# Pooled keys of a fused attention and ResMLP kernel: TensorE products replaced by transposing transfers and VectorE column sums from the third batch on

## The chip, the cores and the metric

The kernel runs on one core of one Trainium2 chip. A core has five engines, each with its own instruction queue: TensorE (PE; its weight loads, PEld, overlap its products), VectorE (DVE), ScalarE (ACT), GpSimd (POOL) and SyncE (SP), which here only issues transfers. Each queue is worked off in its order, and an instruction whose inputs are not there holds up what is queued behind it. Transfers are moved by 16 DMA engines. Those that SP (and at a few places ACT) issues stand in the profile under queue q1, those that POOL issues under q0. The metric is device time in microseconds (us), lower is better.

## The reference

Attention over pooled keys and values, and behind it a ResMLP block on the same tokens. There are 8 batches, 8 heads, 576 tokens and head size 64, in float32; eight neighbouring tokens of k and v are averaged, which leaves 72 groups.

```python
# attention: q, k, v are (8, 8, 576, 64)
k_p = k.reshape(B, H, 72, 8, D).mean(axis=3)
v_p = v.reshape(B, H, 72, 8, D).mean(axis=3)
scores = scale * np.matmul(q, k_p.transpose(0, 1, 3, 2))
attn = softmax(scores)                       # written out: max, exp, sum
x = np.matmul(attn, v_p)                     # then (B, S, H * D)
# ResMLP: d_model 512, hidden 2048
a1 = alpha1 * x + beta1
tok = np.einsum('ts,bsd->btd', w_tok, a1)
u = x + lam * tok
a2 = alpha2 * u + beta2
out = u + lam * (np.maximum(a2 @ w_ch1, 0.0) @ w_ch2)
```

## The kernel before

**Blocks.** All tokens of all batches are cut into 36 chunks of 128 tokens, and four chunks make a block, so there are nine blocks n = 0 to 8 (the loop at line 1127). Block n does the two large products of the MLP on its 512 tokens: `mlp_A` (line 838: 16 pieces, each four products of 128x512, then ReLU on ACT) and, from block 2 on, `product` (line 945, with half-width columns and sums of hidden parts, `hidden_sum` on DVE) and `gather` (line 976, DVE). Between these pieces the attention and the token mixing of batch b = n + 1 are spread out (`attention(b)`, line 1076).

**Order.** Nothing schedules this at run time. Each step of a block is put in a list with a number, the list is sorted by it (line 1205), and the steps are written to the engines' queues in that order. One unit is about one piece of `mlp_A` on TensorE; a block has some 30 units. So a step with 28.5 stands near the end of its block, one with 0.2 at the start of it.

**Keys of a batch, from batch 1 on.** `load_k` (line 275) loads four heads at a time: 512 tokens a head, four neighbouring tokens in one partition. `sum_k` (line 368) adds the four on POOL with two instructions, `k_raw` (line 372) and `k_bf` (line 374), and writes the sum twice side by side, so that two copies of a head fill 128 columns. `att_K` (line 624) then pools pairs of partitions and transposes at once by products with a constant matrix: for each half of the heads (u = 0, 1) four products of line 632 and, for the last 64 tokens, two of line 638, into a PSUM bank of the ring `gp` (six banks, used in turn for nearly everything). DVE copies the bank to SBUF as `kp` (line 644). In the list, `sum_k` stands at -0.9 and 0.3 and `att_K` at 4.1 and 6.1.

**The last 64 tokens** of q and k come with `load_rem` (line 328). `cast_rem` (line 351, on POOL, at 23.1 of the block before) makes bfloat16 copies `rem_q` and `rem_k`; where batches are loaded into reused memory a one-column DVE memset (line 355) stands ahead of them. `att_Frem` (line 603, at 26.72) transposes `rem_q` by a transfer into one of two buffers `rem_qT`.

**Scores.** `att_S4` (line 689) stands at 6.3 for u = 0 and at 13.6 for u = 1. Its products (lines 700 and 707) need `kp`, the transposed queries `qT` (a transfer, line 584) and `rem_qT`. ACT takes the exponentials (line 729, scale 0.125), `att_AV` (line 733) multiplies with the pooled v, and DVE divides (lines 749 and 751), which frees the bank.

**Other users of the SP queue.** `mix_uT` (line 813) transposes each finished chunk `u_bf` to `u_fm` by a transfer (line 820). A block with an odd batch has a fifth such chunk, near unit 27.4; it belongs to the block after the next. `store` (line 880) writes four chunks of the output, at 27.2 (two) and 29.2 (two). `load_v` (line 340, at 3.5 and 7.5), `load_rem` and `load_k` (near 21) fetch the next batch. POOL issues the loads of `q_bf` (line 266) at 0.4 and 0.5 for batches 4 to 7, so just behind `sum_k`.

**Memory reused.** `wt_bf` (the token weights as loaded) is dead once its transposes are made; `scale_w2` (line 898) takes its place for the first of four parts of the scaled second MLP weight. `kpT_pool` is used by batch 0 alone.

Of the kernel before, what the change touches and what calls it, by code (L numbers as in the profile page):

```python
# [7 lines left out]
FP = mybir.dt.float32  # L8
F16 = mybir.dt.float16
BF = mybir.dt.bfloat16  # L10
AF = mybir.ActivationFunctionType
ALU = mybir.AluOpType
AX = mybir.AxisListType

P = 128
SPG = 72
DM = 512
# [171 lines left out]
def direct(  # L189
# [19 lines left out]
    nc = tc.nc  # L209
    ctx.enter_context(tc.manual_schedule())  # L210
    B, H, S, D = q.shape

    const = ctx.enter_context(tc.tile_pool(name="const", bufs=1))
    work = ctx.enter_context(tc.tile_pool(name="work", bufs=1))
# [3 lines left out]
    def gp(name):  # L218
        return psA.tile([P, 512], FP, tag="gp", name=name)
# [29 lines left out]

        nc.vector.tensor_reduce(out=fine, in_=every, op=ALU.min, axis=AX.X)  # L250

    st1 = {}

    def new_batch(b):
        st1[b] = {"qT": [None] * 2, "ET": [None] * H, "raw": [None] * 2, "q": [None] * 2,
# [94 lines left out]

    def cast_rem(b, eng, copy=None, behind=None):
        raw = st1[b]["rem_raw"]
        rq = work.tile([P, 2, 2, D], BF, tag="rem_q", bufs=2, name="rem_q")
        if behind is not None:
            behind.memset(rq[:, 0, 0, 0:1], 0.0)
        rk = work.tile([P, 2, 2 if b else 3, D], BF, tag="rem_k", bufs=2, name="rem_k")
        (copy or eng.tensor_copy)(out=rq.rearrange("p c h d -> p h c d"), in_=raw[:, 0])
        twice = [raw[:, 1, :, c].unsqueeze(2).to_broadcast((P, 2, 2, D)) for c in range(2)]
        if b:
            eng.tensor_tensor(out=rk, in0=twice[0], in1=twice[1], op=ALU.add)  # L360
        st1[b]["rem"] = rq, rk

    def cast_rem_k(eng):
        raw, rk = st1[0]["rem_raw"], st1[0]["rem"][1]
# [3 lines left out]
    def sum_k(b, u, eng):  # L368

        raw = st1[b]["raw"][u]  # L370
        bf = work.tile([P, 4, 2, D], BF, tag="k_bf", bufs=2, name="k_bf")
        eng.tensor_tensor(out=raw[:, :, 0:2], in0=raw[:, :, 0:2], in1=raw[:, :, 2:4], op=ALU.add)  # L372
        twice = [raw[:, :, c].unsqueeze(2).to_broadcast((P, 4, 2, D)) for c in range(2)]
        eng.tensor_tensor(out=bf, in0=twice[0], in1=twice[1], op=ALU.add)  # L374
        st1[b]["k"][u] = bf


    wt_bf = const.tile([P, 5 * S + 64], BF, tag="wt_bf", name="wt_bf")
# [63 lines left out]
    load_wtok()  # L442

    vp1_pool, kpT_pool, kp_pool, ET_pool = [], [], [], []
    for i in range(4):
        if i < 2:
            t = const.tile([SPG, 4, 66], F16, tag=f"vp1_{i}", name=f"vp1_{i}")
            nc.vector.memset(t, 8.0)
            vp1_pool.append(t)
            t = const.tile([P, 2, 4, SPG], BF, tag=f"kpT_{i}", name=f"kpT_{i}")  # L450
            nc.vector.memset(t, 0.0)
            kpT_pool.append(t)
            kp_pool.append(const.tile([P, 4, SPG], BF, tag=f"kp_{i}", name=f"kp_{i}"))
    for i in range(2):
        t = const.tile([SPG, 4, S + 64], F16, tag=f"ET_{i}", name=f"ET_{i}")
        nc.vector.memset(t[:, :, S:], 1.0)
# [9 lines left out]
                            in1=pool_v[0:32, 1:16:2], op=ALU.add)  # L466
# [136 lines left out]
    def att_Frem(b, copy=None):  # L603

        st = st1[b]
        st["rem_qT"] = work.tile([P, 2, P], BF, tag="rem_qT", bufs=2, name="rem_qT")
        if copy is None:
            nc.sync.dma_start_transpose(out=st["rem_qT"],
                                        in_=st["rem"][0].rearrange("p c h d -> p (c h d)"))
            return  # L610
        ps_q = gp("ps_qr").bitcast(BF)
        for c in range(2):
            nc.tensor.transpose(out=ps_q[:, 128 * c:128 * c + 128],
                                in_=st["rem"][0][:, c].rearrange("p h d -> p (h d)"),
                                identity=identity_bf)
        copy(out=st["rem_qT"], in_=ps_q[:, 0:256].rearrange("p (c t) -> p c t", c=2))
# [7 lines left out]
    def att_K(b, u, copy):  # L624

        st = st1[b]
        ps_kp = gp("ps_kp")
        kp = ps_kp[:, 0:4 * SPG].rearrange("p (h g) -> p h g", g=SPG)
        n, nr = (1, 1) if b else (4, 2)
        for h in range(4):  # L630
            for c in range(n):
                nc.tensor.matmul(  # L632
                    out=kp[:, h, 0:64],
                    lhsT=st["k"][u][:, h, c:c + 2].rearrange("p a d -> p (a d)"),
                    rhs=pool_main, start=(c == 0), stop=(c == n - 1))
        for hh in range(2):
            for c in range(nr):
                nc.tensor.matmul(
                    out=kp[:, hh:4:2, 64:72],
                    lhsT=st["rem"][1][:, hh, c:c + 2].rearrange("p a d -> p (a d)"),  # L640
                    rhs=pool_rem.rearrange("p (g u r) -> p u r g", r=2, u=2)[:, u],
                    start=(c == 0), stop=(c == nr - 1))
        if b:
            copy(out=kp_pool[u], in_=kp)
            return
        for a in range(2):
            rows = slice(64 * a, 64 * a + 64)
            (copy or (nc.scalar.copy, nc.vector.tensor_copy)[a])(
                out=kpT_pool[u][rows, a], in_=kp[rows])

    def first_V(b, u, copy=nc.vector.tensor_copy):

# [36 lines left out]
    def att_S4(b, u):  # L689

        st = st1[b]
        qT, kp, rest = st["qT"][u], kp_pool[u], st["rem_qT"]
        lo = [psB.tile([P, DM], FP, tag="ch", bufs=2, name="ps_s") for _ in range(2)]
        hi = [gp("ps_s") for _ in range(2)]
        r = [gp("ps_r")[0:SPG, 0:128].rearrange("p (h i) -> p h i", i=64) for _ in range(2)]

        def main(i):
            for a in range(2):
                rows = slice(64 * a, 64 * a + 64)
                nc.tensor.matmul(  # L700
                    out=(hi if i > 1 else lo)[a][0:SPG, 256 * (i % 2):256 * (i % 2) + 256],
                    lhsT=kp[rows, i, :], rhs=qT[rows, 2 * i:2 * i + 2, :])

        def rests(i):
            for a in range(2):
                rows = slice(64 * a, 64 * a + 64)
                nc.tensor.matmul(  # L707
                    out=r[a][:, i // 2], lhsT=kp[rows, i + a, :],
                    rhs=rest[rows, :, 2 * u + i // 2::4].rearrange("p c i -> p i c"))

        pairs = ((lo, 0), (hi, 2)) if u else ((hi, 2), (lo, 0))
        main(pairs[0][1])
        rests(pairs[0][1])
        main(pairs[0][1] + 1)
        main(pairs[1][1])
        rests(pairs[1][1])
        main(pairs[1][1] + 1)
        ET = ET_pool[u]
        for i in range(4):
            st["ET"][4 * u + i] = ET[:, i]  # L720

        def exp(k):
            if k < 2:
                o, i = ET[:, k::2, 512:S], r[k]
            else:
                a, (pair, h) = k % 2, pairs[k // 2 - 1]
                o = ET[:, h:h + 2, 256 * a:256 * a + 256]
                i = pair[a][0:SPG, :].rearrange("p (h i) -> p h i", i=256)
            nc.scalar.activation(out=o, in_=i, func=AF.Exp, bias=0.0, scale=0.125)  # L729

        st["exp", u] = exp

# [158 lines left out]

    FIRST = 2
    HALF = DM // 2
    wino = {}

    w2l = {}

    def scale_w2(g, i):

        if g not in w2l:  # L900
            if g == 1:
                both = const.tile([P, 6 * DM], BF, tag="vecs", name="w2_l")
                w2l[1] = both[:, 0:4 * DM].rearrange("p (i d) -> p i d", d=DM)
                wino["spare"] = both[:, 4 * DM:].rearrange("p (j t) -> p j t", t=HALF)
            else:
                w2l[g] = const.tile([P, 4, DM], BF, tag=("wt_bf", None, "w2_0", "w2_1")[g],
                                    name="w2_l")
        nc.vector.tensor_tensor(out=w2l[g][:, i], in0=w2[g][:, i], in1=lam_bc, op=ALU.mult)

    def weight_sum(i, g):  # L910
# [92 lines left out]
    more_constants()  # L1003
    keep_warm(1)
    att_Frem(0, nc.scalar.copy)
    keep_warm(1)
    spread_lam()
    double_k(0)
    att_K(0, 0, None)
    spread_al1(0)  # L1010
    bias_row(0)
# [64 lines left out]
    def attention(b):  # L1076


        first = b == 1
        todo = []  # L1080
# [11 lines left out]
            todo.append((25.6 if first else 23.1, lambda: cast_rem(b + 1, nc.gpsimd, behind=None if first else nc.vector)))  # L1092
            todo.append((26.72 if b > 1 else 26.22, lambda: att_Frem(b + 1)))
        for u in range(2):
            todo.append((3.6 + 0.1 * u if first else -0.9 + 1.2 * u,
                         lambda u=u: sum_k(b, u, nc.gpsimd)))
            todo.append((7.0 + 2.3 * u if first else 4.1 + 2.0 * u,
                         lambda u=u: att_K(b, u, nc.vector.tensor_copy)))
        for u in range(2):
            at = (9.0 if first else 6.3, 13.6)[u]  # L1100
            todo.append((at, lambda u=u: att_S4(b, u)))
# [3 lines left out]
            for i, dt in enumerate((2.9, 3.4, 4.6, 5.1) if u else early):  # L1105
                h = 4 * u + i
                todo.append((at + dt, lambda h=h: att_AV(b, h)))
                if i % 2:
                    eng = nc.gpsimd if h == 5 or first and h < 5 else nc.vector
# [17 lines left out]
    for n in range(NBLK):  # L1127
        todo = []
# [60 lines left out]
        b = n + 1  # L1189
# [61 lines left out]
```

## Time and profile before

The median of three runs is 333.19 us (333.13 to 333.4). The profiled execution took 332.3 us; the span from its first to its last instruction is 330.6 us, and times in the views count from the span's start. The granted TensorE clock reads 1.00 in it.

| what | instructions | one, ns | busy, us |
|---|---|---|---|
| DVE, all | 490 | | 235.5 (71% of the span) |
| ACT, all | 322 | | 175.5 (53%) |
| POOL, all | 110 | | 95.6 (29%) |
| L632 products `ps_kp` of `k_bf` | 56 | 193 | 3.9 |
| L638 products `ps_kp` of `rem_k` | 36 | 178 | 3.4 |
| L644 DVE `kp` <- `ps_kp`, 128x288 | 14 | 451 | 6.3 |
| L372 POOL `k_raw`, 128x512 | 14 | 1338 | 18.7 |
| L374 POOL `k_bf`, 128x512 | 14 | 1318 | 18.5 |
| L820 SP transposing issue `u_fm` | 32 | 1212 (median) | |
| L584 SP transposing issue `qT` | 12 | 1284 (median) | |
| L608 SP transposing issue `rem_qT` | 6 | 1196 (median) | |

Products are pipelined, so the mean duration of one is not what it takes of TensorE's time; that is read from the distance between starts. The duration of an SP issue is the time that the SP queue is held, not the time until the data has landed. q1 moved 32.67 MB in 52,236 packets, q0 12.40 MB in 13,824.

In the profiled execution the blocks n = 1 to 7 begin on TensorE at 67.7, 102.9, 137.8, 171.5, 206.4, 240.0 and 274.9 us; the block that begins at 137.8 us carries the attention of batch 4.

### The profile page before, as it was taken

How to read it: one execution, taken by the hardware profiler on the slowest of the kernel's cores; microseconds unless marked ns; L12 is line 12 of the kernel's file. 1: busy time of each engine (PE TensorE's matmuls, PEld its weight loads, DVE VectorE, ACT ScalarE, POOL GpSimd, SP SyncE). 2: the span in 40 equal slices, each digit the busy share in tenths (PEclk: the TensorE clock that was granted, in tenths of full speed). 3: DMA queues.
4: the chain of work that ended last, by engine and by line, in shares of the span. 5: the costliest groups of instructions: out<-in, count | busy, mean ns of one | idle time of the engine just before them, and what ended most of it. 6: DMA issues, size and time to landing. Idle time of an engine off the chain costs nothing.

```text
span 330.6 us, 6522 instructions
## 1 busy us (share of the span) xinstructions
PE 324.9 (98%) x2528; PEld 208.9 (63%) x2528; DVE 235.5 (71%) x490; ACT 175.5 (53%) x322; POOL 95.6 (29%) x110
## 2 busy tenths in 40 slices
PE   8999999999999999999999999999999999999995
PEld 3667764455545576656775677557755866586584
DVE  6674389999589969776967796878688783265263
ACT  2775989458323852387128812782268225803710
POOL 8769738301256011700290028102610200000000
PEclk9999999999999999999999999999999999999999
DMA  8999999959894982499549934995340044003003
GB/s 119 193 219 270 268 210 249 207 145 124 165 255 68 221 203 59 76 227 165 164 119 201 171 125 89 207 195 157 65 136 2 0 65 143 2 0 129 2 32 97
DMA packets 66618, 45.83 MB, mean 139 GB/s; under 512 B 34541, under 2 KB 57205, under 8 KB 66586
## 3 DMA queue, kind: packets, MB, share of 16 engines
q1 hardware_dynamic: 52236, 32.67, 42.6%
q0 software_dynamic: 13824, 12.40, 22.9%
q8 instruction: 20, 0.33, 0.4%
q10 hardware_dynamic: 526, 0.34, 0.3%
q14 instruction: 12, 0.10, 0.1%
HBM read 38.30 MB, written 9.44 MB: 144 GB/s over the span
## 4 chain that ended last, share of the span: by engine, by line
PE 98%; DVE 1%; issue 0%; ACT 0%
PE ps_h L849 38%; PE ps_w L972 26%; PE ps_tok L801 12%; PE ps_ch L869 8%; PE ps_av L743 3%; PE ps_s L700 2%; PE ps_warm L792 2%; PE ps_kp L632 1%; PE ps_r L707 1%; PE ps_av L747 1%; PE ps_q L589 1%; PE ps_sc L680 0%; PE ps_rs L528 0%; PE ps_w L516 0%; PE ps_uT L825 0%; PE ps_v L659 0%
## 5 line engine op out<-in xcount | busy, mean ns | idle before, releaser
L849 PE MATMUL ps_h<-u_fm,w 128*128 128x512 bf16 (+2 forms) x608 | 133.7, 369 | 0.2 <-DVE bias_cols L852 0.2
L856 ACT ACTIVATE H<-ps_h,bias_cols 128x512 bf16<-128x512 f32 x144 | 98.1, 688 | 56.5 <-PE ps_h L849 55.5
L849 PEld LDWEIGHTS <-w 128*128 128x128 bf16 x608 | 65.8, 114 | 49.7 <-issue 2.2
L972 PEld LDWEIGHTS <-H 128*128 128x128 bf16 x560 | 53.4, 98 | 10.9 <-DVE u_sb L990 1.2
L809 ACT CAST u_bf<-u_sb 128x512 bf16<-128x512 f32 x32 | 19.8, 618 | 70.0 <-issue 39.9
L972 PE MATMUL ps_w<-w_l,H 128*128 128x256 bf16 x448 | 53.6, 273 | 0.0
L990 DVE TENSOR_TENSOR u_sb<-u_sb,ps_w 128x512 f32<-128x512 f32 x54 | 36.3, 682 | 17.0 <-PE ps_w L972 17.0
L765 POOL TENSOR_TENSOR xs<-x_tm,lamal_bc 128x512 bf16<-128x512 f32 x12 | 15.9, 1330 | 108.8 <-DVE x_tm L751 108.6
L801 PE MATMUL ps_tok<-xs,wtT 128*128 128x512 bf16 (+3 forms) x200 | 44.9, 381 | 0.1
L805 DVE TENSOR_TENSOR u_sb<-x_tm,ps_tok 128x512 f32<-128x512 f32 (+1 forms) x40 | 27.3, 683 | 9.9 <-PE ps_tok L801 9.9
L751 DVE TENSOR_TENSOR x_tm<-ps_av,recs 128x320 f32<-128x320 f32 x64 | 31.5, 492 | 2.6
L729 ACT ACTIVATE ET<-ps_s 72x512 f16<-72x512 f32 x56 | 32.3, 591 | 0.0
L801 PEld LDWEIGHTS <-wtT 128*128 128x128 bf16 (+3 forms) x200 | 17.4, 100 | 16.2 <-issue 1.1
L749 DVE RECIPROCAL recs<-ps_av 128x5 f32<-128x5 f32 x64 | 12.1, 188 | 16.7 <-PE ps_av L747 16.6
L670 DVE TENSOR_TENSOR v_u<-v_u 72x1024 f32<-72x1024 f32 (+1 forms) x24 | 22.7, 948 | 0.2
L972 PE MATMUL ps_w<-w_t,h_s 128*128 128x256 bf16 x168 | 22.6, 273 | 0.0
L869 PEld LDWEIGHTS <-H 128*128 128x128 bf16 x128 | 11.9, 98 | 13.7 <-issue 0.4
L372 POOL TENSOR_TENSOR k_raw<-k_raw 128x512 f32<-128x512 f32 x14 | 18.7, 1338 | 1.2 <-PE ps_ch L869 0.7
L972 PEld LDWEIGHTS <-h_s 128*128 128x128 bf16 x168 | 16.4, 98 | 4.1
L941 DVE TENSOR_TENSOR H<-H,H 128x1024 bf16<-128x1024 bf16 x14 | 9.7, 690 | 12.8 <-ACT H L856 12.7
L374 POOL TENSOR_TENSOR k_bf<-k_raw 128x512 bf16<-128x512 f32 x14 | 18.5, 1318 | 1.1
L743 PEld LDWEIGHTS <-ET 72*128 72x128 f16 x256 | 14.0, 97 | 6.0 <-DVE vp L664 0.3
(153 smaller groups left out, 369.3 us busy)
## 6 DMA issues: line engine op xcount, KB each, us to landing
out_dram<-u_sb SPq DMA_DIRECT2D x29, 256.0 KB
k_raw<-in_k_dram SPq DMA_DIRECT2D x12, 512.0 KB
v_u<-in_v_dram SPq DMA_DIRECT2D x12, 512.0 KB
q_bf<-in_q_dram POOLq DMA_DIRECT2D x16, 256.0 KB, 7.4
w<-in_moe_w_ch_dram POOLq DMA_DIRECT2D x6, 512.0 KB, 12.9
out_dram<-u_sb SPq DMA_DIRECT2D x11, 128.0 KB
w<-in_moe_w_ch_dram POOLq DMA_DIRECT2D x1, 1024.0 KB, 14.3
k_raw<-in_k_dram POOLq DMA_DIRECT2D x2, 512.0 KB, 16.7
```

Of the source, the lines that this page charges most:

```text
L670: nc.vector.tensor_tensor(out=out, in0=t[:, :, 0:width], in1=t[:, :, width:2 * width], op=ALU.add)
L729: nc.scalar.activation(out=o, in_=i, func=AF.Exp, bias=0.0, scale=0.125)
L743: nc.tensor.matmul(out=av[:, odd + c, :], lhsT=ET[:, m0:m0 + 128], rhs=vp1[:, h % 4, :])
L751: nc.vector.tensor_tensor(out=x[:, 1 - odd:6 - odd, dd:dd + D], in0=av[:, :, 0:64], in1=rec.unsqueeze(2).to_broadcast((P, 5, D)), op=ALU.mult)
L801: nc.tensor.matmul(out=ps_tok[p0:p1], lhsT=wtT[0:kk, at, P * c:P * c + p1 - p0], rhs=xs_pool[i][0:kk, sc, :], start=(sc == 0), stop=(sc == 4))
L805: nc.vector.tensor_tensor(out=s["u"][p0:p1, :], in0=x[p0:p1, 1 + c if c < 4 else 5 - 5 * i, :], in1=ps_tok[p0:p1, 0:DM], op=ALU.add)
L809: nc.scalar.copy(out=s["u_bf"], in_=s["u"])
L849: nc.tensor.matmul(out=ps_h[:, t0:t1 + one], lhsT=w1_of(cc, j), rhs=rhs, start=(cc == 0), stop=(cc == 3))
L856: nc.scalar.activation(out=H4[n, j // 4][:, j % 4, :], in_=ps_h, func=AF.Relu, bias=bias_cols[:, j:j + 1], scale=1.0)
L869: nc.tensor.matmul(out=ps, lhsT=H_of(n, j)[:, 128 * m:128 * m + 128], rhs=(w2l if n else w2)[j // 4][:, j % 4, :], start=(j == 0), stop=(j ...
L972: nc.tensor.matmul(out=ps, lhsT=stat(j), rhs=moving(j), stop=(j == 7), start=(first and (pp == 0 or alone) and j == 0), skip_group_check=True)
L990: nc.vector.tensor_tensor(out=o, in0=o, in1=banks[key, "both"], op=ALU.add)
```

## The change

From batch 2 on, `att_K` is no longer called. In its place:

- `att_KT` transposes the four-token sums `k_bf` of half the heads (128x512) by a transfer on SP, into the old `kpT_pool` memory. u = 0 stands at 28.5 of the block before, u = 1 at 0.2 of the batch's own block.
- `att_Ksum` (DVE, at 4.3 and 6.3) adds neighbouring columns of it and writes `kp`.
- `cast_rem` writes the last tokens of q and k side by side, and one transfer in `att_Frem` transposes both (512 columns, where it was 256) into a single buffer beside the scaled weight in the old `wt_bf` memory.
- `att_Krest` (POOL, two instructions at 0.25) adds the eight last-token groups into `kp` for all heads.
- `sum_k` of batch b + 1 now stands at 28.1 and 28.2 of the block before. On POOL's queue it keeps its place behind `cast_rem`; `att_Krest` comes between it and the issue of the `q_bf` loads.
- The pooled keys are sums and not means, and the factor 1/8 goes into the scale of the exponentials.

In the queue of SP the transposes of `att_KT` stand so: at the change to batches 4 and 6 behind three stores (two of them of half a chunk) and the fifth `u_fm`, then two stores, then u = 1; at the change to batches 5 and 7 behind two stores, then two stores, then u = 1; at the change to batch 3 right behind `att_Frem`, then two stores, then u = 1; at the change to batch 2 between the two transposes of `qT`, and u = 1 behind two stores. In all of these the loads of v follow.

```diff
     def cast_rem(b, eng, copy=None, behind=None):
-        rq = work.tile([P, 2, 2, D], BF, tag="rem_q", bufs=2, name="rem_q")
+        both = work.tile([P, 5, 2 * D], BF, tag="rem_qk", bufs=2, name="rem_qk")
...
     def att_Frem(b, copy=None):
+        if copy is None:
+            both = wino["rem_T"].rearrange("p (x t) -> p x t", t=P)
+            nc.sync.dma_start_transpose(out=both, in_=st["rem"][2])
+            st["rem_qT"], st["rem_kT"] = both[:, 0:2], both[:, 2:4]
+            return
...
+    def att_KT(b, u):
+        nc.sync.dma_start_transpose(out=quads_of(u),
+                                    in_=st1[b]["k"][u].rearrange("p h a d -> p (h a d)"))
+
+    def att_Krest(b, eng):
+        pairs = st1[b]["rem_kT"].rearrange("p e (r i a) -> p (e r) i a", i=2, a=8)
+        half = wino["half"].bitcast(FP).rearrange("p (e a) -> p e a", a=8)
+        eng.tensor_tensor(out=half, in0=pairs[:, :, 0], in1=pairs[:, :, 1], op=ALU.add)
+        eng.tensor_tensor(
+            out=kp_both[:, :, 64:72].rearrange("p (a e) r -> p e r a", e=2),
+            in0=half[:, :, 0:4].rearrange("p (e r) a -> p e r a", e=2),
+            in1=half[:, :, 4:8].rearrange("p (e r) a -> p e r a", e=2), op=ALU.add)
+
+    def att_Ksum(b, u):
+        quads = quads_of(u).rearrange("p h (g i) -> p h g i", i=2)
+        nc.vector.tensor_tensor(out=kp_pool[u][:, :, 0:64], in0=quads[:, :, :, 0],
+                                in1=quads[:, :, :, 1], op=ALU.add)
...
-            nc.scalar.activation(out=o, in_=i, func=AF.Exp, bias=0.0, scale=0.125)
+            nc.scalar.activation(out=o, in_=i, func=AF.Exp, bias=0.0,
+                                 scale=0.125 if b == 1 else 0.125 / 8)
...
         for u in range(2):
-            todo.append((3.6 + 0.1 * u if first else -0.9 + 1.2 * u,
-                         lambda u=u: sum_k(b, u, nc.gpsimd)))
-            todo.append((7.0 + 2.3 * u if first else 4.1 + 2.0 * u,
-                         lambda u=u: att_K(b, u, nc.vector.tensor_copy)))
+            if first:
+                todo.append((3.6 + 0.1 * u, lambda u=u: sum_k(b, u, nc.gpsimd)))
+                todo.append((7.0 + 2.3 * u, lambda u=u: att_K(b, u, nc.vector.tensor_copy)))
+            else:
+                todo.append((4.3 + 2.0 * u, lambda u=u: att_Ksum(b, u)))
+            if b < B - 1:
+                todo.append((28.1 + 0.1 * u, lambda u=u: sum_k(b + 1, u, nc.gpsimd)))
+        if b < B - 1:
+            todo.append((28.5, lambda: att_KT(b + 1, 0)))
+        if not first:
+            todo.append((0.2, lambda: att_KT(b, 1)))
+            todo.append((0.25, lambda: att_Krest(b, nc.gpsimd)))
```

More of the change, by code (lines that the diff above doesn't have):

```diff
@@ L250, in count_in_range @@
         nc.vector.tensor_reduce(out=fine, in_=every, op=ALU.min, axis=AX.X)
-    st1 = {}
+    st1, wino = {}, {}
     def new_batch(b):
@@ L352, in cast_rem @@
         raw = st1[b]["rem_raw"]
-        rq = work.tile([P, 2, 2, D], BF, tag="rem_q", bufs=2, name="rem_q")
+        both = work.tile([P, 5, 2 * D], BF, tag="rem_qk", bufs=2, name="rem_qk")
         if behind is not None:
-            behind.memset(rq[:, 0, 0, 0:1], 0.0)
-        rk = work.tile([P, 2, 2 if b else 3, D], BF, tag="rem_k", bufs=2, name="rem_k")
+            behind.memset(both[:, 0, 0:1], 0.0)
+        rq = both[:, 0:2].rearrange("p c (h d) -> p c h d", h=2)
+        flat = both.rearrange("p x d -> p (x d)")
+        n = 4 if b else 6
+        rk = flat[:, 4 * D:(4 + n) * D].rearrange("p (h a d) -> p h a d", h=2, a=n // 2)
         (copy or eng.tensor_copy)(out=rq.rearrange("p c h d -> p h c d"), in_=raw[:, 0])
@@ L360, in cast_rem @@
             eng.tensor_tensor(out=rk, in0=twice[0], in1=twice[1], op=ALU.add)
-        st1[b]["rem"] = rq, rk
+        st1[b]["rem"] = rq, rk, flat[:, 0:8 * D]
     def cast_rem_k(eng):
@@ L444, in direct @@
     vp1_pool, kpT_pool, kp_pool, ET_pool = [], [], [], []
+    kp_both = const.tile([P, 8, SPG], BF, tag="kp", name="kp")
     for i in range(4):
@@ L452, in direct @@
             kpT_pool.append(t)
-            kp_pool.append(const.tile([P, 4, SPG], BF, tag=f"kp_{i}", name=f"kp_{i}"))
+            kp_pool.append(kp_both[:, 4 * i:4 * i + 4])
     for i in range(2):
@@ L605, in att_Frem @@
         st = st1[b]
+        if copy is None:
[3 more added lines that the diff above has]
+            return
         st["rem_qT"] = work.tile([P, 2, P], BF, tag="rem_qT", bufs=2, name="rem_qT")
[L607 to L610, printed above, removed]
         ps_q = gp("ps_qr").bitcast(BF)
@@ L649, in att_K, with quads_of @@
                 out=kpT_pool[u][rows, a], in_=kp[rows])
+    def quads_of(u):
+        return kpT_pool[u].rearrange("p a h g -> p (a h g)")[:, 0:512].rearrange(
+            "p (h t) -> p h t", t=P)
+    def att_KT(b, u):
[13 more added lines that the diff above has]
+                                in1=quads[:, :, :, 1], op=ALU.add)
     def first_V(b, u, copy=nc.vector.tensor_copy):
@@ L893, in direct @@
     HALF = DM // 2
-    wino = {}
     w2l = {}
@@ L904, in scale_w2 @@
                 wino["spare"] = both[:, 4 * DM:].rearrange("p (j t) -> p j t", t=HALF)
-            else:
-                w2l[g] = const.tile([P, 4, DM], BF, tag=("wt_bf", None, "w2_0", "w2_1")[g],
-                                    name="w2_l")
+            elif g == 0:
+                both = const.tile([P, 4 * DM + 6 * P], BF, tag="wt_bf", name="w2_l")
+                w2l[0] = both[:, 0:4 * DM].rearrange("p (i d) -> p i d", d=DM)
+                wino["rem_T"] = both[:, 4 * DM:4 * DM + 4 * P]
+                wino["half"] = both[:, 4 * DM + 4 * P:]
+            else:
+                w2l[g] = const.tile([P, 4, DM], BF, tag="w2_%d" % (g - 2), name="w2_l")
         nc.vector.tensor_tensor(out=w2l[g][:, i], in0=w2[g][:, i], in1=lam_bc, op=ALU.mult)
```

## The prediction

> **What bounds the kernel now.** I read the page's shares first, then the chain of work that ended last around one change of batch, then the queues of SP and DVE there, and last what the DMA engines moved in the same microseconds. Part 1 and part 4 of the page:
>
> ```profile
> PE 324.9 (98%) x2528; PEld 208.9 (63%) x2528; DVE 235.5 (71%) x490; ACT 175.5 (53%) x322; POOL 95.6 (29%) x110
> PE 98%; DVE 1%; issue 0%; ACT 0%
> ```
>
> TensorE is busy for 98% of the span and is 98% of the chain. What is taken from its queue shortens the run, and a wait put into it lengthens the run, one for one, unless something covers it. The chain from 137 to 148 us (start, length, what), where batch 4's attention begins:
>
> ```profile
> 137.84 4.32 PE ps_h L849 x20
> 142.16 0.12 PE ps_kp L632 x4
> 142.27 0.05 PE ps_kp L638 x2
> 142.32 1.74 PE ps_h L849 x8
> 144.06 0.12 PE ps_kp L632 x4
> 144.18 0.04 PE ps_kp L638 x2
> 144.22 0.23 PE ps_s L700 x2
> ```
>
> The pooling products hold TensorE for 0.16 us twice per batch, and the first score product follows at 144.22 us. There are no gaps, so nothing waits for keys now: `k_bf` was done on POOL by 137.4 us. The SP timeline there (start, time that the queue is held), and POOL's issue of the q loads:
>
> ```profile
> 136.85 1.21 SPq L889 DMA_DIRECT2D out_dram<-u_sb  x2
> 138.10 0.58 SPq L885 DMA_DIRECT2D out_dram<-u_sb  x1
> 138.78 1.61 SPq L820 DMA_TRANSPOSE u_fm<-u_bf  x1
> 140.49 1.02 SPq L885 DMA_DIRECT2D out_dram<-u_sb  x2
> ```
> ```profile
> 137.38 1.57 POOL L266 DMA_DIRECT2D q_bf<-in_q_dram  x2
> ```
>
> The transpose of `u_bf` issued at 138.78 us is of the size of a k transpose, 128x512. When does its data move? The DMA view of 139 to 143 us, then of 143 to 146 us (packets, MB, share of 16 engines):
>
> ```profile
> DMA packets 829, 0.69 MB, mean 174 GB/s; under 512 B 48, under 2 KB 637, under 8 KB 829
> q0 software_dynamic: 605, 0.30, 67.8%
> q1 hardware_dynamic: 224, 0.39, 36.3%
> ```
> ```profile
> DMA packets 1091, 0.55 MB, mean 184 GB/s; under 512 B 560, under 2 KB 995, under 8 KB 1091
> q1 hardware_dynamic: 640, 0.33, 65.3%
> q0 software_dynamic: 451, 0.22, 58.6%
> ```
>
> A 128x512 transpose is 128 KB, and the small packets come in lots that fit 512 packets of 256 B for each. Up to 143 us only 48 small ones passed; the 560 came from 143 to 146 us. So this transpose needed about 7 us from issue to the end of its data, behind the stores ahead of it in q1 and beside the q loads of q0. Without such traffic (133.6 to 136.2 us) 1083 small packets passed in 2.6 us at 50.1% of the engines: 0.6 to 0.7 us of pure transfer for 512. At the change to batch 6 it is the same: from 207.3 to 211.8 us q0 moved 1020 packets and q1 99, 40 of them small; the `u_fm` issued at 207.99 us moved from 211.8 to 213.0 us (569 small ones). Today nobody needs this chunk for a whole block, so the delay costs nothing. DVE's queue:
>
> ```profile
> 142.36 0.46 DVE L644 CAST kp<-ps_kp 128x288 bf16<-128x288 f32 x1 [0.88 <-PE ps_kp L638]
> 144.47 0.45 DVE L644 CAST kp<-ps_kp 128x288 bf16<-128x288 f32 x1
> 146.68 0.69 DVE L941 TENSOR_TENSOR H<-H,H 128x1024 bf16<-128x1024 bf16 x1 [0.71 <-ACT H L856]
> ```
>
> Between the second `kp` and the first reciprocal of `att_AV` (148.01 us) DVE has 0.71 us of idle time, later 0.40 us; that is all the slack in which it can be late.
>
> **The change, part by part.** *Removed from TensorE:* 2 x 0.16 us in each of six batches, 1.9 us, all on the chain. *DVE:* a copy of 0.45 us becomes an add of 128x256 in bfloat16; the nearest row is the 72x256 add of L670, 420 ns: no difference. It no longer waits for TensorE but for a transfer. *POOL:* two adds of 128 and 64 columns; rows near them are 400 ns (128x256 cast, L357) and 450 ns (64x128 add, L758): 0.7 us a batch. POOL then waits 17 us or more for DVE (its rows of L765), so this is hidden, but the issue of the q loads behind it starts 0.7 us later. The last-token transfer lands before: it was issued at 134.97 us, and POOL is free at 137.4 us. *SP:* two more transposing issues of 1.2 us a batch. Behind them stand the v loads, `qT`, `load_rem` and `load_k` of the next batch. The k loads of batch 5 were issued by 159.1 us and POOL used them at 166.84 us, where it had been waiting for a DVE memset until 165.79 us: a delay of 2.4 us is hidden; without this cover it would move `sum_k` and the next k transposes by as much. *DMA:* 1280 more small packets a batch, 1.6 us of all engines, spread over 34 us. *`sum_k`:* moved in the list, but not in POOL's queue: nothing. Exponentials: same count.
>
> *The new wait.* It decides, and differs by batch. Batches 2 and 7 have no q loads at their start (the page's q0 is silent from 240 to 246 us); the last `qT` of batch 2 was issued by 69.5 us and the scores come at 74.1 us, so three more issues still fit: 0 each. Batch 4: the u = 0 transpose is queued right behind `u_fm`. Its data can follow when that is through, at about 146.0 us; add 0.65 us of its own, some 0.3 us until it is reported, 0.42 us for the add: scores at 147.3 us, against 143.9 us without the pooling products: TensorE idle for 3.4 us. The q loads now come 0.7 us later, which lets some stores pass first, and may also push `u_fm` back by as much. Bounds: 0 (all passes ahead of the q loads) and 4.1; I take 2.8, nearer the row that the transfer follows. Batch 6: 213.0 + 1.4 = 214.4 us against 212.4 us; bounds 0 and 2.7, I take 1.7. Batches 3 and 5: u = 0 goes ahead of the q loads, but u = 1 stands behind two stores that then crawl. From 172 to 180 us q1 moved 697 packets in all beside q0's 1033. I place the u = 1 data at 180.3 us, 2.1 us after DVE reached its copy (178.08 us); behind it wait the v sums, `hidden_sum` and the division of `att_AV`. Less 0.71 and 0.36 us of DVE slack there and about 0.3 us until a bank is missed, TensorE loses 0.8 us; bounds 0 and 2. For batch 3 the same 0.8. In batches 4 and 6 the first wait covers the second.
>
> Sum: -1.9 + 2.8 + 1.7 + 0.8 + 0.8 = +4.2 us. The profiled execution took 332.3 us (span 330.6), so 336.5 us; the median of the runs lies 0.9 us above it, so the forecast is **337.4 us**. With every wait at 0 it is 331.3 us, with every wait at its upper bound (4.1 + 2.7 + 2 + 2 - 1.9 = 8.9) 342.1 us.
>
> The row above of 1020 q0 packets against 99 is what the queueing rests on. [...]
>
> **The rivals.** *Hidden, 331.3 us, faster:* all transposes land before their adds. For: the q loads start later, and 7 us passed only where two queues met. Against: SP cannot issue before `u_fm` is issued (140.4 us), and q0 would be under way by 139.8 us. It decides if the data of batch 4's u = 0 is in by 143.2 us. *Partly hidden, 333 us:* only one of the four waits is as priced (2 us). *The clock falls, 342.8 us:* the waits of batches 4 and 6 are long enough for TensorE to come back at half clock. In this trace the clock rows read 0.5 until 6.84 us and 1.0 after, with products from 1.39 us on: 5.45 us at half speed lose 2.7 us, and two such waits add 5.4 us to 337.4. [...] Against: no idle stretch of that length occurs here, so nothing shows the fall. [...] *The change does not do what it says:* TensorE's queue loses 144 entries, 72 products and their loads, so no.
>
> **How the numbers follow.** Chances: forecast 0.54 (its own range 334.5 to 341), hidden 0.26, partly hidden 0.10, clock 0.10. A measurement here tells 0.2%, 0.7 us, from no change: faster 0.28, same 0.07, slower 0.65 (the partly hidden case is shared out). The range reaches from the hidden case to the upper bounds, 331.0 to 342.3 us; the clock case and the tails are left out.
>
> **What would show it.** The L632 row falls from 56 to 8 instructions and L638 from 36 to 12. Right: TensorE idle ahead of the first score products of batches 4 and 6 (2.8 and 1.7 us), the DVE add in front of it released by a transfer of `kpT`; none in batches 2 and 7; DVE waiting for u = 1 in 3 and 5. Wrong: a chain without gaps there and a span near 328.7 us. Prediction wrong upwards: clock rows below 1.0 behind these gaps, or v and k loads late by the longer SP queue.

## The result, and the profile after

The changed kernel takes 347.3 us (median of 6 runs, 345.44 to 353.33), the kernel before beside it 333.16 us (332.06 to 337.38). The ratio is 1.0422, 95% interval 1.0388 to 1.0457: slower by 14 us, where 4.2 us were forecast. The ratio leaves out the slow run at 353.33 us. The profiled execution of the changed kernel took 347.5 us, span 345.7 us, 15.1 us more than the span before.

Parts 1, 2 and 4 of its page, and the rows of part 5 for the new add and the score products (busy time, mean ns | idle time before them and what ended it):

```profile
PE 325.3 (94%) x2425; PEld 207.4 (60%) x2456; DVE 236.2 (68%) x490; ACT 175.8 (51%) x322; POOL 102.9 (30%) x122
...
PEclk9999999999999999989999899999999999999999
...
PE 68%; DVE 13%; DMA 12%; issue 2%; POOL 2%; SPq 1%; ACT 0%; POOLq 0%; DVEq 0%
...
L730 PE MATMUL ps_s<-qT,kp 64*72 64x256 bf16 x112 | 12.9, 296 | 7.2 <-DVE kp L678 6.1
...
L678 DVE TENSOR_TENSOR kp<-kpT 128x256 bf16<-128x256 bf16 x12 | 5.1, 422 | 20.5 <-DMA kpT<-k_bf 20.5
```

TensorE's busy time is as before (325.3 against 324.9 us, some of it at a lower clock); it now covers 94% of the span, and transfers make up 12% of the chain. VectorE waited 20.5 us for the transposing transfers of `k_bf`, and TensorE 6.1 us for VectorE's adds. Two slices of PEclk read 8.

Where the time went is best seen block by block: the distance on TensorE from the first product of one `mlp_A` pass to that of the next, in us, in the two profiled executions. The fourth column is the first experiment, in which no add waits.

| block with the attention of | before | after | adds read a constant | after less constant |
|---|---|---|---|---|
| batch 2 | 35.21 | 37.19 | 34.95 | 2.24 |
| batch 3 | 34.91 | 36.60 | 34.57 | 2.03 |
| batch 4 | 33.62 | 37.89 | 33.29 | 4.60 |
| batch 5 | 34.91 | 38.42 | 34.57 | 3.85 |
| batch 6 | 33.62 | 36.80 | 33.29 | 3.51 |
| batch 7 | 34.91 | 34.57 | 34.57 | 0.00 |
| sum | | | | 16.23 |

The chain of the changed kernel at the start of batch 4 (start, length, what):

```profile
143.89 0.61 SPq L851
144.50 0.05 issue
144.55 0.02 SPq L662
144.57 0.03 issue
144.60 6.36 DMA kpT<-k_bf
150.96 0.02 issue
150.98 0.44 DVE kp L678
151.42 0.14 issue
151.56 0.43 PE ps_s L730 x2
```

The chain runs through the SP queue: the issue of the fifth `u_fm` (L851), the issue of the transposing transfer (L662), 6.36 us until that has landed, the add, the scores. TensorE's last product before them ended at 148.34 us, so it idled for 3.22 us. In batch 5 the second transfer is the one; VectorE's timeline (start, length, idle time before it in brackets):

```profile
183.74 0.41 DVE L678 TENSOR_TENSOR kp<-kpT 128x256 bf16<-128x256 bf16 x1
184.40 0.69 DVE L975 TENSOR_TENSOR h_s<-H 128x1024 bf16<-128x1024 bf16 x1 [0.24 <-ACT H L887]
185.01 1.21 DVE L700 TENSOR_TENSOR v_u<-v_u 72x1024 f32<-72x1024 f32 x1
190.92 0.42 DVE L678 TENSOR_TENSOR kp<-kpT 128x256 bf16<-128x256 bf16 x1 [4.70 <-DMA kpT<-k_bf]
191.26 0.68 DVE L700 TENSOR_TENSOR v_u<-v_u 72x512 f32<-72x512 f32 x1
```

The first add starts at once, the second waits 4.70 us, and the v sums, the MLP's `h_s` and the division of `att_AV` queue behind it; TensorE then misses 1.70 and 0.30 us. The transfer was issued at 183.42 us and landed 7.47 us later. The DMA view of 186 to 189 us shows what it shared the engines with:

```profile
DMA packets 1154, 0.45 MB, mean 151 GB/s; under 512 B 521, under 2 KB 1154, under 8 KB 1154
...
q0 software_dynamic: 649, 0.32, 105.4%
q1 hardware_dynamic: 505, 0.13, 38.4%
```

q0 is the q load that POOL had issued at 182.8 us. The transfer's 512 packets of 256 B pass from 186.1 to 189.4 us among the packets of that burst (185.0 to 192.5 us, 95% of them by 190.0), not ahead of it.

Last, the clock. The windows view, in steps of 3.4 us around the gaps of batches 4, 5 and 6 (busy time of each engine with its count, then the granted clock, the share of the DMA engines and GB/s):

```profile
147.80:151.20 3.40, 0.54 (x3) 0.06 (x1) 0.22 (x1) 1.08 (x2) 0.00 (x0) 1.00 1.37 240
151.20:154.60 3.40, 3.04 (x17) 1.68 (x18) 2.87 (x5) 0.92 (x3) 0.00 (x0) 0.50 1.10 231
192.10:195.50 3.40, 1.40 (x16) 0.76 (x14) 3.26 (x8) 1.01 (x2) 0.00 (x0) 1.00 0.63 148
195.50:198.90 3.40, 3.18 (x18) 1.46 (x18) 3.21 (x9) 1.61 (x4) 0.00 (x0) 0.51 1.17 154
222.80:226.20 3.40, 1.85 (x9) 0.76 (x7) 0.00 (x0) 2.06 (x3) 0.00 (x0) 1.00 1.35 191
226.20:229.60 3.40, 2.05 (x19) 1.30 (x20) 2.16 (x3) 1.16 (x4) 0.00 (x0) 1.00 1.16 242
```

TensorE comes back at half clock for 3.4 us behind batch 4's gap and again behind batch 5's, but not behind batch 6's.

### The profile page after: what moved, and what is told of

Read it like the earlier page. It is cut to its first block, busy times and chain, and to the rows that moved or that the text cites. A ratio compares the mean times of both kernels' runs of the same rounds, so it can differ in the third digit from the quotient of the medians.

```text
span 345.7 us, 6382 instructions
## 1 busy us (share of the span) xinstructions
PE 325.3 (94%) x2425; PEld 207.4 (60%) x2456; DVE 236.2 (68%) x490; ACT 175.8 (51%) x322; POOL 102.9 (30%) x122
## 4 chain that ended last, share of the span: by engine, by line
PE 68%; DVE 13%; DMA 12%; issue 2%; POOL 2%; SPq 1%; ACT 0%; POOLq 0%; DVEq 0%
PE ps_w L1006 25%; PE ps_h L880 21%; PE ps_tok L832 10%; DMA kpT<-k_bf 9%; PE ps_ch L900 6%; DMA wt_bf<-in_moe_w_tok_dram 3%; DVE x_tm L782 2%; DVE v_u L700 2%; DVE w_l L942 2%; PE ps_av L774 2%; PE ps_s L730 1%; DVE xs L796 1%; DVE u_sb L836 1%; DVE vp L700 1%; DVE kp L678 1%
## 5 line engine op out<-in xcount | busy, mean ns | idle before, releaser
L880 PEld LDWEIGHTS <-w 128*128 128x128 bf16 x608 | 66.5, 115 | 54.2 <-issue 3.9
L730 PE MATMUL ps_s<-qT,kp 64*72 64x256 bf16 x112 | 12.9, 296 | 7.2 <-DVE kp L678 6.1
L678 DVE TENSOR_TENSOR kp<-kpT 128x256 bf16<-128x256 bf16 x12 | 5.1, 422 | 20.5 <-DMA kpT<-k_bf 20.5
```

The source lines that it names most:

```text
L880: nc.tensor.matmul(out=ps_h[:, t0:t1 + one], lhsT=w1_of(cc, j), rhs=rhs, start=(cc == 0), stop=(cc == 3))
```

## The experiments

### The waits taken away, all and by halves

The adds of `att_Ksum` read a constant tile in place of the transposed sums; every transfer, SP issue and POOL add stays. The pooled keys of batches 2 to 7 are then not those of k. First for both halves of the heads, as shown, then for u = 1 alone, then for u = 0 alone (`if u == 1`, `if u == 0`).

```diff
     def att_Ksum(b, u):
         quads = quads_of(u).rearrange("p h (g i) -> p h g i", i=2)
+        if True:
+            quads = identity_bf.unsqueeze(1).to_broadcast((P, 4, P)).rearrange(
+                "p h (g i) -> p h g i", i=2)
```

> The changed kernel with every transfer, POOL add and DVE add left in place, but the DVE add reads a constant tile instead of the transposed sums, so it waits for no transfer (the pooled keys of batches 2 to 7 are then not those of k). Theory A, the loss is the wait of the add for its transfer and what follows from it: 331.3 us, each of blocks 1 to 6 of the trace 0.3 us shorter than before the change. Theory B, the transfers themselves (longer SP queue, traffic, POOL adds) delay other work: 340 us or more, with gaps at other lines.

Measured: 331.18 us, ratio to before 0.9947 (0.9923 to 0.9972); the blocks are in the table above, no idle time on TensorE between them, clock 1.0. Its page:

```profile
PE 320.7 (98%) x2425; PEld 206.2 (63%) x2456; DVE 235.8 (72%) x490; ACT 175.2 (53%) x322; POOL 102.7 (31%) x122
```

So the whole loss comes from the adds' wait for the transfers. The extra transfers, the longer SP queue and POOL's adds cost nothing by themselves, and the removed products save 1.9 us (0.26 to 0.34 us a batch).

> As the first, but only the add of the second half of the heads (u = 1) reads a constant tile. Theory A with the second transfer as the larger part: only batches 4 and 6 still idle in front of their first scores (3.2 and 2.9 us in the changed kernel), with one stretch of half clock: about 338 us. If the first transfers were the main loss: 344 us or more. Theory B: 345 us.

> Only the add of the first half of the heads (u = 0) reads a constant tile; u = 1 waits as in the change. Theory A: batches 2, 3 and 5 lose what they lose in the change (2.0, 1.7 and 3.5 us in blocks 1, 2 and 4), batches 4 and 6 about 2 us each through the second half: about 342 us. If u = 1 costs nothing: 333 us.

Measured: 340.87 us where only the first add waits (one run), 347.59 us where only the second does (one run). Against the kernel with no wait, the first adds alone cost batch 4 5.05 and batch 6 4.22 us; the second adds alone cost batch 3 3.74, batch 4 4.08, batch 5 2.66 and batch 6 6.68 us. (Batch 2 took 0.82 us more in the first of these runs, but not by its transfer, which had landed at 72.6 us, 1.6 us ahead of the add: TensorE waited 0.7 us for ACT's `H`.) The second adds alone lose as much as the changed kernel does: in batches 4 and 6 the two waits lie on top of each other, and taking away the first one moves the stop from the first scores to the second half. The falls of the clock lie elsewhere in this run, behind 118.3 and 155.9 us and for 6.8 us behind 230.9 us, so a single block can differ from the changed kernel's by what a fall costs. Both runs came out above what was expected of them, the second by most.

### q's loads kept away

Theory from here on: the transposing transfers are late because q's loads for the next batch run beside them on POOL's queue. First try, by the list alone:

```diff
-                    at = {1: 11.0, 2: 6.5}.get(b, 0.4) + 0.1 * u
+                    at = {1: 11.0, 2: 6.5}.get(b, 9.0) + 0.1 * u
```

(with `att_F` of b + 1 at 18.0 in place of 10.0 for b over 2).

> The changed kernel with the loads of q for batches 4 to 7 issued at unit 9.0 of the block instead of 0.4, and their transposes at 18.0 instead of 10.0; nothing else moves. Theory A with the q loads as what holds q1: blocks 2, 4 and 5 fall to 0.3 us under the kernel before, block 3 too, only block 1 (no q loads there) keeps its 2.0 us: about 333.5 us. If the stores ahead in the same queue hold the transposes by themselves: no better than 343 us.

Measured: 348.76 us, ratio 1.0486 (1.045 to 1.0522). It tested nothing: the issues left at 107.18 and 143.27 us, where the changed kernel's left at 107.07 and 142.98 us. POOL has no other work there, so a later place in the list does not delay it. The load has to wait for something, as it already does in batch 2's block, where a one-column VectorE memset of the tile stands ahead of it. On top of the edit above:

```diff
                     todo.append((at, lambda b=b, u=u: load_q_bf(
-                        b + 1, u, nc.vector if b == 2 else None)))
+                        b + 1, u, nc.vector if b > 1 else None)))
```

> The order on SP's queue is that of the changed kernel; only q's loads of batches 4 to 7 are held back, by a VectorE memset of one column in front of each at some 9 us into the block instead of the block's start. Theory A1 (the transfers are slow because q's loads, 1 KB packets on POOL's queue, run beside their 256-byte packets): the waits of batches 3, 4, 5 and 6 fall to what batch 2 shows, where no q load runs (about 2 us each, or none), so 333 to 339 us. Rival A2 (they are slow because they are issued late, behind u_fm and the stores, and q's loads only share the time): the second add's wait falls little, the sum stays within 2 us of the changed kernel's 347.3.

Measured: 333.83 us, ratio 1.0023 (0.9998 to 1.0048). (q's packets are of 512 B, 0.32 MB in 649 in the view above, not of 1 KB.) The order on SP's queue is unchanged, and 13.5 us are gone. The SP timeline at the start of batch 4, and VectorE's:

```profile
140.19 1.26 SPq L851 DMA_TRANSPOSE u_fm<-u_bf  x1
141.54 1.21 SPq L662 DMA_TRANSPOSE kpT<-k_bf  x1
142.84 1.00 SPq L916 DMA_DIRECT2D out_dram<-u_sb  x2
143.94 1.21 SPq L662 DMA_TRANSPOSE kpT<-k_bf  x1
```
```profile
144.03 0.43 DVE L678 TENSOR_TENSOR kp<-kpT 128x256 bf16<-128x256 bf16 x1 [1.17 <-DMA kpT<-k_bf]
...
146.54 0.42 DVE L678 TENSOR_TENSOR kp<-kpT 128x256 bf16<-128x256 bf16 x1 [0.35 <-DMA kpT<-k_bf]
```

The same places behind `u_fm` and stores, but the transfers issued at 141.54 and 143.94 us have landed when the adds start, at 144.03 and 146.54 us: 2.5 and 2.6 us, where they took 6.4 and 6.0. Batches 3, 4, 5 and 7 have the times of the kernel without waits; batch 6 keeps 1.2 us and batch 2, in which no q load runs, 2.2 us. In both of these the second transfer still takes 4.4 to 4.5 us, for a cause of its own that is taken up with batch 2 below. Theory A1 holds, and A2 falls: at the same places behind `u_fm` and the stores the other transfers of batches 3 to 7 land in 2.4 to 2.8 us.

The dose: only the second of the two q loads is held back, so that half the burst stays (and the second `att_F` of b + 1 goes back by 8 units for b over 2).

```diff
-                    at = {1: 11.0, 2: 6.5}.get(b, 0.4) + 0.1 * u
+                    at = {1: 11.0, 2: 6.5}.get(b, 9.0 if u else 0.4) + 0.1 * u
...
-                        b + 1, u, nc.vector if b == 2 else None)))
+                        b + 1, u, nc.vector if b == 2 or b > 2 and u else None)))
```

> As the run with all q loads held back, but only the second q load of batches 4 to 7 is (a VectorE memset at some 9 us into the block); the first still leaves at the block's start. So the burst beside the transposing transfers is half as long. Theory D (a transposing transfer lands when the q burst ends, so its time is set by the size of the burst): u = 1 of batches 3 and 5 lands some 3.5 us earlier than in the changed kernel (7.5 us after its issue becomes 4), u_fm and u = 0 of batches 4 and 6 likewise; batch 3 loses its wait, batch 5 keeps about 1 us of it on VectorE, batches 4 and 6 keep 1 to 2 us each, and the time is 335 to 339 us. Rival E (any q traffic on POOL's queue costs the transfer the same, a fixed price at the start of a burst): the transfers still take 6 to 7 us and the time is 345 us or more.

Measured: 338.37 us, ratio 1.0169 (1.0139 to 1.0198). The chain in batch 5:

```profile
178.83 6.19 DMA kpT<-k_bf
185.02 0.02 issue
185.05 0.43 DVE kp L678
```

The last packets of this half burst start at 112.8, 146.3, 184.0 and 216.8 us in batches 3 to 6, and the first transfer of k still under way there lands at 113.6, 147.3, 185.0 and 217.8 us, 0.8 to 1.1 us behind. The second transfers of batches 4 and 6, two stores further back, land 3.8 us behind the burst. Theory D holds in its main point: these landings follow the end of the burst, and a shorter burst ends sooner. The expected gain in landing time was too large (6.2 us in batch 5, not 4), because q's first packet starts some 2 us after POOL's issue (1.8 to 2.4 us in the changed kernel) and half a burst still takes 2.4 to 3.6 us. Batch 5 alone would fit the 6 to 7 us of rival E; the 3.8 to 4.8 us of batches 4 and 6, where the full burst gave 6.0 to 6.6, do not, and the time is within the 335 to 339 us given, not 345.

### The transfers put ahead

Both transfers of a batch right behind that of the last tokens, ahead of the fifth `u_fm` and all stores; q's loads as in the changed kernel.

```diff
-                todo.append((28.1 + 0.1 * u, lambda u=u: sum_k(b + 1, u, nc.gpsimd)))
+                todo.append((28.1 if first else 26.74, lambda u=u: sum_k(b + 1, u, nc.gpsimd)))
...
-            todo.append((28.5, lambda: att_KT(b + 1, 0)))
+            for u in range(2):
+                todo.append((28.55 if first else 26.8 + 0.01 * u, lambda u=u: att_KT(b + 1, u)))
         if not first:
-            todo.append((0.2, lambda: att_KT(b, 1)))
```

> Both transposing transfers of a batch's sums of k stand right behind the one of its last tokens on SP's queue, ahead of the fifth u_fm and the four stores of the block, and the sums on POOL stand two places earlier; everything else is the changed kernel. Theory A (the loss is the place on the queues: the transfers are issued last, so that they land beside q's loads and behind u_fm and stores): both land before the batch begins, no VectorE add waits, TensorE has no gap ahead of the first scores, and the time is that of the kernel whose adds read a constant, 331 us, so some 1.5 us under the kernel before. Rival B (the transfers themselves disturb the others: small packets in front of the fifth u_fm and the stores cost as much): the wait goes over to u_fm, whose matmuls then begin late in batches 4 and 6, and the time is 334 to 340. Rival C (such a transfer takes 7 us wherever it stands): second adds still wait in batches 3 and 5 only if issued less than 7 us ahead; they are issued some 9 us ahead, so C too gives 331, and the landing times tell it from A: 2.4 us by A, 7 by C.

Measured: 330.64 us (330.38 to 331.73), ratio to before 0.9936 (0.9914 to 0.9957). This version beats both kernels, the one before by 0.6%. SP's timeline ahead of batch 4, VectorE's first add there, and the DMA view of 135.5 to 139.2 us:

```profile
134.29 1.19 SPq L612 DMA_TRANSPOSE w_l<-rem_qk  x1
135.57 2.54 SPq L662 DMA_TRANSPOSE kpT<-k_bf  x2
138.20 1.21 SPq L920 DMA_DIRECT2D out_dram<-u_sb  x2
139.45 0.58 SPq L916 DMA_DIRECT2D out_dram<-u_sb  x1
140.13 1.34 SPq L851 DMA_TRANSPOSE u_fm<-u_bf  x1
```
```profile
140.64 0.41 DVE L678 TENSOR_TENSOR kp<-kpT 128x256 bf16<-128x256 bf16 x1
```
```profile
DMA packets 1622, 0.39 MB, mean 106 GB/s; under 512 B 1622, under 2 KB 1622, under 8 KB 1622
...
q1 hardware_dynamic: 1622, 0.39, 52.2%
```

All small packets have passed by 139.2 us with nothing from q0 beside them, and the add has no wait in brackets. Both land 2.4 us after their issue in every batch. Rival B falls too: `u_fm` lands 6.2 us after its issue in batch 4 (7.5 before the change, 138.78 to 146.25 us) and 6.7 us in batch 6 (5.4 before), and nobody waits for it. Rival C falls with the 2.4 us.

> Only the second transposing transfer of each batch is moved, from the start of the next block to right behind the first, so that it passes two of the four stores and is issued some 2 to 4 us earlier; the first stays where it is. Theory A (place on the queue): batches 2, 3 and 5, whose first transfer lands in 2.4 us with no wait, lose their wait: 347.3 - 2.3 - 2.0 - 3.8 = 339 us; batches 4 and 6, whose first transfer waits behind the fifth u_fm, keep theirs. Rival (the second takes 7 us whenever q's loads come within that time): batches 3 and 5 keep a wait of 1 to 2 us each, 341 to 344 us.

```diff
-            todo.append((28.5, lambda: att_KT(b + 1, 0)))
+            for u in range(2):
+                todo.append((28.5 + 0.01 * u, lambda u=u: att_KT(b + 1, u)))
         if not first:
-            todo.append((0.2, lambda: att_KT(b, 1)))
```

Measured: 343.88 us, one run. Its first full block began 4.3 us later than that of the kernel without waits (31.3 against 27.0 us; the clock reads 0.5 from 11 to 25 us), which no edit touches; the blocks say what the move did. Batches 2, 3, 5 and 7 have the times without a wait, batches 4 and 6 keep 4.94 and 4.12 us. Without the late start the run would be at 339.6 us, the 339 of theory A. The second transfer is issued 1.3 to 2.0 us behind the first, where it was 2.4 to 4.1, so 1.1 to 2.5 us earlier. In batch 3 it landed ahead of the burst; in batch 5 it met the burst's first 2 us, landed after 4.1 us, and its add waited 0.19 us.

> Both edits: the two transposing transfers stand first, and q's loads of batches 4 to 7 are held back by a VectorE memset until some 9 us into the block (their own transposing transfers at 18 instead of 10). Theory A: nothing waits in either, so the same time as with the transfers first alone, 331 us within 0.5, or up to 1 us more if q's later landing makes its own transposing transfers collide with k's loads at 21. If the transfers first alone still waits on q's loads somewhere, this one is the faster by that wait.

Measured: 332.06 us (330.78 to 335.46), ratio 0.9977 (0.994 to 1.0013): both edits together bring nothing over the first, as expected; three of its ten runs took 335.3 to 335.5 us. In its profiled execution the first block begins at 31.0 us behind the same early stretch of half clock, and from batch 3 on its blocks are equal to those of the kernel with the transfers first, to 0.01 us.

### The clock's part

14 products of 128x512 without use fill TensorE's gap ahead of the first scores of batches 4 and 6; nothing else changes.

```diff
+            if u == 0 and b in (4, 6):
+                todo.append((at - 0.01, lambda: fill_gap(14)))
             todo.append((at, lambda u=u: att_S4(b, u)))
```

> The changed kernel with 14 products without use (identity times a weight, 128x512, some 3.0 us) put in front of the first scores of batches 4 and 6 on TensorE, where it idles for 3.22 and 2.90 us. They move no other instruction and leave all transfers. Theory (part of the loss of batch 4 is the clock: half speed for 3.4 us behind the gap, which costs 1.7 us): the clock rows show no 0.5 behind batch 4, its block of TensorE falls from 37.89 to 36.2 us, batch 6's stays at 36.8 since there was no fall of the clock, and the whole is 345.6 us; the fall behind batch 5 (gap of 1.70 us) stays. Rival (the clock falls whatever TensorE does there, or the loss is waiting only): block 4 stays at 37.9.

Measured: 346.89 us, one run; batch 4's block fell from 37.89 to 36.57 us. The windows around it:

```profile
147.10:150.50 3.40, 3.40 (x17) 1.37 (x14) 0.29 (x1) 1.01 (x2) 0.00 (x0) 1.00 1.40 232
150.50:153.90 3.40, 3.15 (x23) 1.86 (x24) 3.28 (x7) 2.23 (x6) 0.00 (x0) 1.00 1.09 231
```

The clock stays at 1.00 behind it. The first scores start 9.43 us into the block in this run and in the changed kernel, so the whole difference lies behind them: the fall had cost this block 1.3 us (1.7 expected), the wait itself the other 3.3 us. That the products kept the clock up is likely, not shown by this one run: if its changes of the clock also lie whole steps of 3.41 us apart, as the four in the changed kernel's trace do (1, 12 and 1 steps), one can stand 13 steps back from its fall at 193.9 us, at 149.5 us, and the gap from 147.4 to 150.8 us would have been cut in two (an estimate). The fall behind batch 5 stayed, and batch 6's block got longer, not shorter (37.56 us): there no clock was to be had, and its transfer landed later (7.4 us after its issue, not 6.1). Batch 2 lost its wait in this run, which is taken up below.

## Why the prediction was right and wrong

- **Removed products, 1.9 us: right.** 0.26 to 0.34 us in each of six batches, 1.9 us in all.
- **VectorE's add, POOL's adds, SP's issues, more packets, `sum_k` moved, each at nothing: right.** The kernel whose adds read a constant has them all and takes 331.18 us, where 331.3 us was worked out for the case without waits.
- **Batch 7, no wait: right.** 34.57 us with and without the wait.
- **The four waits together:** each came out above its upper bound, 4.60 against 4.1 us in batch 4, 3.51 against 2.7 in batch 6, 2.03 and 3.85 against 2 in batches 3 and 5.
- **Batch 4, 2.8 us (0 to 4.1): mechanism right, size short.** The add's wait ended with the transfer queued behind the fifth `u_fm`; the gap was 3.22 us, close to the 3.4 us that the working had found and then shaded down. The block lost 4.60 us, the rest with the fall of the clock. The working's 0.3 us until a transfer is reported stand in no row: in the trace before, this `u_fm` landed 0.5 us after its last packet of 256 B (145.73 to 146.25 us), in the changed kernel batch 5's second transfer 1.5 us after (189.43 to 190.89 us).
- **Batch 6, 1.7 us (0 to 2.7): mechanism right, size short.** The gap was 2.90 us and the block lost 3.51 us. The working had the transfer pass right behind `u_fm`; `u_fm` was through at 223.6 us, and the transfer landed only behind the end of q's burst, at 227.0 us (the last q packet starts at 226.2).
- **Batches 3 and 5, 0.8 us each (0 to 2): the step that failed most.** "I place the u = 1 data at 180.3 us", 8.8 us into batch 5's block; it landed 10.9 us into the changed kernel's (190.89 us, the block began at 180.0). The wait on VectorE was 4.70 us, not 2.1; TensorE lost 2.0 us in gaps, and the block 3.85 us, of which the 3.4 us at half clock behind them can make up to 1.7. Batch 3 lost 2.03 us. The placing counted packets of q1; but the transfer's own packets only began to pass at 186.1 us, behind the stores and among q's, and were through at 189.4, the 4-byte packets behind them at 189.6. The row for it stood in the prediction: 7 us from issue to landing for the transpose of `u_bf` beside q's load. It was used for batch 4 and not for the second transfers.
- **Batch 2, 0: wrong, 2.24 us.** No q load runs there, which was right. The second transfer still took 4.4 us. In the run with q held back its small packets are through by 75.0 us, and the DMA view of 74.8 to 77 us shows one packet more:

```profile
q1 hardware_dynamic: 109, 0.02, 5.1%
q8 instruction: 1, 0.02, 2.8%
```

A 16 KB packet of the instruction queue starts at 75.1 us and holds one DMA engine for 0.97 us; two of the transfer's 4-byte packets come behind it, at 76.1 us, and the add starts at 77.2 us. In the changed kernel the packet starts at 76.1 us and it is the same. In two runs it missed the transfer: in the run with the gaps filled it started at 76.6 us, when the transfer was landing (76.7 us, 2.6 us after its issue), and batch 2 took 34.88 us; in the run where only u = 1 waits it started at 74.5 us, and the transfer landed at 74.6 us, 2.65 us after its issue. In all six profiled runs with the second transfer at this place and the packet at 75.1 to 76.1 us it took 4.2 to 4.4 us. Batch 6 of the run with q held back shows the same: the packet starts at 213.9 us, two 4-byte packets come at 214.9 us, and the add starts at 216.1 us. No experiment moved the packet alone, so this rests on these coincidences.
- **"In batches 4 and 6 the first wait covers the second": right in the kernel as it is** (0.53 and 0.81 us of VectorE's wait were left), but a cover only: with the first wait gone the second costs as much.
- **The rival with the clock** was told apart from the forecast, and both happened. It had priced each fall at 2.7 us for two batches; a fall is 3.4 us at half speed, 1.3 us in batch 4, and the second came behind batch 5. The 2.7 us came from the first 6.84 us of the trace before, where the windows view reads 1.00; the products show about half the pace there: 13 of 128x512 (line 792) in 5.66 us, 0.44 us each, where 20 of line 849 took 4.32 us, 0.22 us each. That an idle stretch brings the clock down was shown by nothing ahead of the result. In the changed kernel's trace the clock falls at 151.17 and 195.54 us and is back at 154.58 and 198.95 us, so the four changes lie 3.41, 40.96 and 3.41 us apart: 1, 12 and 1 steps of 3.41 us. An idle stretch of that length was not needed for it: the 3.4 us ahead of the second fall held 1.40 us of products.
- **The queueing.** The prediction rested it on 1020 q0 packets to 99 of q1, ten to one. In batch 5's burst, from 186 to 189 us, the rows read 649 to 505, so ten to one is no fixed share, and a burst cannot be costed by it.

The forecast's sum was -1.9 + 6.1 us; measured it is -1.9 + 16.2 us, and 0.7 us at the start, 15.0 of the 15.1 us between the spans. Of the 10 us that were missed, batches 3 and 5 make 4.3, batch 2 2.2, batches 4 and 6 3.6, and up to 3 us of these are the two falls of the clock.

## What to carry to other kernels

Here a transfer that takes 2.4 us alone took 6.0 to 7.5 us when it met another queue's burst. The first one in its queue landed from 1.6 us ahead of the burst's last packet to 0.8 us behind it, one queued two stores further back some 3.6 us behind. So cost a new transfer on a path that matters by its landing beside that traffic, and give every such transfer that price, not just the one with a row to show it. The cure is cheap once the cause is known: the late transfers, issued two to six microseconds earlier, turn a loss of 4.2% into a gain of 0.6%. And a step put later in a list delayed nothing on an engine that had no other work (q's loads left at 107.18 us instead of 107.07); it needs something to wait for.

## What had not been expected of the hardware

- In the changed kernel the clock fell after stretches of 3.4 us in which TensorE was busy for 0.54 and 1.40 us, and stayed up after stretches with 1.85 and 2.05 us. A gap of 2.90 us (224.65 to 227.55 us), which lies across the last two of these, cost no clock; one of 1.70 us (192.71 to 194.41 us), with one of 0.30 us behind it in the same stretch, did. No threshold follows from this: in the run where only u = 1 waits the clock also fell after a stretch with 1.85 us (114.89 to 118.30 us).
- One 16 KB packet of the instruction queue, 0.97 us long, put back the landing of a 128 KB transfer by some 1.7 us (4.4 us against 2.65), as far as the coincidences above show.
